# Moving row statistics, two attention loads and two weight splits to other steps of a hand-ordered layer kernel

## The chip, the cores and the metric

The kernel runs on one core of a Trainium2 chip. The core has five engines that work side by side, each through its own list of instructions in order: TensorE (PE, matrix products; PEld is its weight load), VectorE (DVE), ScalarE (ACT), GpSimd (POOL) and SyncE (SP), which here does nothing but issue transfers. Transfers are issued from SP's list and from ACT's list, as two queues, and are carried by the same 16 DMA engines. The metric is the device time of one execution in microseconds (us), lower is better; the median over several runs is compared.

## The reference

Input x has 2048 rows of 512 numbers, all float32. What is computed, cut to what matters:

```
xn  = layernorm(x)                                   # per row, no scale
qkv = xn @ wqkv                                      # 512 -> 3*512; 32 heads of 16
logits[s, w] = q[s] . k[s - 2w] / 4,  w = 0..7       # positions before 0 masked
o   = sum_w softmax(logits)[s, w] * v[s - 2w]
att = o @ wo
h   = relu(xn @ w1 + b1) ** 2                        # 512 -> 1792
g   = silu(h @ w2 + b2)                              # 1792 -> 512
out = x + att * g
```

## The kernel before

**Tiles and pairs.** The rows are cut into 16 tiles of 128 rows, which are worked in pairs (a, a+1). The first part of the program (up to about 139 us) makes q, k and v of all tiles; the second part runs the two wide layers over four chunks of 512 rows. The sliding attention of unit u (256 rows, so a pair of tiles) runs on VectorE beside both parts.

**One pair.** Each factor is split into a high and a low part in float32r, so that a product takes three passes. For pairs 4 to 14 the three 256-row products are made from seven products instead of eight, by `pair_of_seven` (L788): in order Q0, T1, T2, Q1, T3, K1, T4, with their partial sums kept in PSUM tiles `pm{a}_0` to `pm{a}_2`; pairs 6 to 12 do the same for half of v (`pv{a}_…`, in between). Pair 14 (the last) does v the plain way and also starts the wide layer (`ph0_0`, `ph0_1`). ScalarE copies each partial sum out before TensorE may add the next product onto it: the copy `pm{a}_1<-pm{a}_0` stands between Q0 and T2, and the copy `stg{a}_0<-pm{a}_0` of T3's result stands between T3 and T4. T1, T2, T3 and K1 use `S{a}_0` and `S{a}_1`, sums of transposed pieces: VectorE makes `Sf{a}`, ScalarE the high part of `S`, VectorE the low part (`low_sums`, L535).

**How a tile gets there.** `spread(t)` (L426) makes the statistics of a tile with two activations of ScalarE (they write a `waste` tile) and three small GpSimd operations; `norm(t)` (L441) then writes the normalised rows `xn`, and after the second tile of a pair `shuffle(t)` (L467) sends the pair through four transfers to `xb`, and loads the x tiles of a later pair. From `xb` VectorE transposes 32x32 blocks into PSUM (`pxT`), ScalarE copies the high part `xt`, VectorE makes the low part.

**What sets the order.** Inside a pair there are six steps; after each, `beside(a, step)` (L764) emits what the table `plan` holds for that place. `slots` (L746) says for each pair t where its statistics and its normalisation stand: four places (a, step), two for `spread` of t and t+1, two for `norm` of t and t+1, the transfers to `xb` with the last. `ahead` (L762) says where the splits of the wide layers' weights (`next_w`, L402: high parts on ScalarE, low parts on GpSimd, then the load of the weights two further on) stand. Every engine keeps program order, so what is emitted first on an engine runs first there. The transfers `sx` (a tile of xt to DRAM for the wide layers) are issued at the head of each pair (L876); `sk`, `sv`, `sq` carry a pair's k, v and q to DRAM from four staging buffers `stg`, so that a staging tile can be filled only when an older store has landed.

**The attention's place.** `attention()` (L248) is a generator that `pump` (L379) advances whenever the program's own clock of VectorE is behind that of TensorE. Its loads of a unit's k, q and v (`load`, L330) come back from DRAM on ACT's queue; they are put off by `defer` until the program's clock has passed a given time, and are emitted at the next `pump`. For unit 0, v's load may follow only from pair 4, step 3 on (`v_ready`).

Of the kernel before, what the change touches and what calls it, by code (L numbers as in the profile page):

```python
# [1 line left out]

# [49 lines left out]

MATMUL, VMATMUL, TRANSPOSE, DVE_FIXED, SHARED, SLACK, LATE, ROOM0, ROOM = 227, 120, 150, 150, 200, 500, 3000, 500, 3500

BEHIND, FAR, FREE, LAND, LOAD = 5000, 9000, 2000, 4500, 10500


@with_exitstack
def body(ctx: ExitStack, tc: tile.TileContext, x, wqkv, wo, w1, b1, w2, b2, out):
# [3 lines left out]
    clock = {"PE": 0.0, "V": 0.0}  # L63
# [30 lines left out]
    PE, V, A, G = Ordered(nc.tensor, "PE"), Ordered(nc.vector, "V"), Ordered(nc.scalar), Ordered(nc.gpsimd)  # L94

    def not_before(t):
        clock["V"] = max(clock["V"], t)
# [119 lines left out]
    def windows(t, i0, dims):  # L217

        part = t[:, i0]
        return bass.AP(tensor=part.tensor, offset=part.offset, ap=[part.ap[0], *dims])  # L220


    done_tiles = {n: [0, {}] for n in "qkv"}
    done_units = [0]

    def load_u(what, u):
        n = BI if what == "q" else WIN
        src = dict(q=sq, k=sk, v=sv)[what]

        t = att.tile([P, n, CH], F32, name=f"{what}{u}", tag="k" if (what, u) == ("v", NU - 1) else what)  # L230
        row = src[0, u * UP:u * UP + 1, :]
        ap = bass.AP(tensor=row.tensor, offset=row.offset, ap=[[BI * CH, NB], [src.shape[1] * CH, GR], [1, n * CH]])
        A.dma_start(t.rearrange("p i c -> p (i c)"), ap)
        return t
# [5 lines left out]
    def defer(t, f):  # L240
        behind.append((t, f))
        behind.sort(key=lambda b: b[0])

    def flush(t):
        while behind and (t is None or behind[0][0] <= t):
            behind.pop(0)[1]()

    def attention():  # L248

        tiles, Ls, landing, exps = {}, {}, {}, set()

        def qk(u, s):
            i0 = 4 * s
            yield from there("k", u)
            yield from there("q", u)
            q, k, L = tiles["q", u], tiles["k", u], Ls[u]
            yield 2350
            pr = att.tile([P, W, 2 * P], F32, name=f"pr{u}_{s}", tag="pr")  # L260
            qv = q[:, i0:i0 + 4, :].rearrange("p i c -> p (i c)")[:, None, :].to_broadcast([P, W, 2 * P])
            V.tensor_mul(pr, windows(k, i0, [[DIL * CH, W], [1, 4 * CH]]), qv)
            yield 2300
            V.tensor_reduce(
                out=L[:, s * 16:(s + 1) * 16, :].rearrange("p m w -> p w m"),
                in_=pr.rearrange("p w (g d) -> p w g d", d=HD), axis=AX.X, op=OP.add)

        def there(n, u):
            while (n, u) not in tiles:
                yield None  # L270
            not_before(landing[n, u])


        def part(u, h):
            n = BI * 4 // 2
            return slice(0, 2 * n) if h is None else slice(h * n, h * n + n)

        def soft_a(u, h=None):
            yield 1500 if h is not None else 700
            m = part(u, h)  # L280
            L, n = Ls[u][:, m], m.stop - m.start
            if u == 0:
                i = slice(m.start // 4, m.stop // 4)
                lm = L.rearrange("p (i h) w -> p i h w", h=4)
                V.tensor_add(lm, lm, mask[:, i, None, :].to_broadcast([P, n // 4, 4, W]))
            mx = att.tile([P, n], F32, name=f"mx{u}_{h}", tag="mx")
            V.tensor_reduce(out=mx, in_=L, axis=AX.X, op=OP.max)
            (G if h is None else V).tensor_sub(L, L, mx[:, :, None].to_broadcast([P, n, W]))

            def exp():  # L290
                A.activation(L, L, AF.Exp, scale=0.25)
                exps.add((u, h))

            defer(clock["V"] + (BEHIND if h is not None else FAR), exp)

        def soft_b(u, h=None):
            while (u, h) not in exps:
                yield None
            yield 2100 if h is not None else 1400
            m = part(u, h)  # L300
            L, n = Ls[u][:, m], m.stop - m.start
            sm = att.tile([P, n], F32, name=f"sm{u}_{h}", tag="sm")
            V.tensor_reduce(out=sm, in_=L, axis=AX.X, op=OP.add)
            V.reciprocal(sm, sm)
            (G if h is None else V).tensor_mul(L, L, sm[:, :, None].to_broadcast([P, n, W]))

        def av(u, s):
            i0 = 4 * s
            yield from there("v", u)
            v, L = tiles["v", u], Ls[u]  # L310
            yield 2400

            pr = att.tile([P, W // 2, 2 * P, 2], F32, name=f"pv{u}_{s}", tag="pr")
            vv = windows(v, i0, [[2 * DIL * CH, W // 2], [DIL * CH, 2], [HD, 16], [1, HD]])
            l = L[:, s * 16:(s + 1) * 16, :].rearrange("p m (a e) -> p a e m", e=2)
            V.tensor_mul(pr.rearrange("p a (g d) e -> p a e g d", d=HD), vv,
                         l[:, :, :, :, None].to_broadcast([P, W // 2, 2, 16, HD]))
            yield 2300
            V.tensor_reduce(
                out=v[:, i0:i0 + 4, :].rearrange("p i c -> p (i c)"), in_=pr.rearrange("p w n e -> p n w e"),  # L320
                axis=AX.XY, op=OP.add)

        def store(u):
            v = tiles.pop(("v", u))
            row = so[0, u * UP:u * UP + 1, :]
            dst = bass.AP(tensor=row.tensor, offset=row.offset, ap=[[BI * CH, NB], [S * CH, GR], [1, BI * CH]])
            dma(dst, v[:, :BI, :].rearrange("p i c -> p (i c)"))
            done_units[0] = u + 1

        def load(u, names):  # L330
            if u == NU:
                return
            for n in names:
                while done_tiles[n][0] < 2 * (u + 1):
                    yield None

                def start(n=n):
                    tiles[n, u] = load_u(n, u)
                    landing[n, u] = clock["PE"] + LOAD

                defer(max(clock["V"] + FREE if u else 0, done_tiles[n][1][u] + LAND), start)

        yield from load(0, "kq")

        for u in range(NU + 1):
            if u < NU:
                Ls[u] = att.tile([P, BI * 4, W], F32, name=f"L{u}", tag="L", bufs=2)
                for s in range(4):
                    yield from qk(u, s)
                    if u == 0 and s % 2:  # L350
                        yield from soft_a(0, s // 2)
                    if u == 0 and s == 1:
                        while not v_ready:
                            yield None
                        yield from load(0, "v")
                if u:
                    yield from soft_a(u)
                yield from load(u + 1, "kq")
                if u == NU - 1:
                    yield from load(u, "v")  # L360
            if u == 0:
                yield from soft_b(0, 0)
            for s in range(4):
                if u > 1 or (u == 0 and s < 2) or (u == 1 and s >= 2):
                    yield from av(max(u - 1, 0), s)
            if u == 0:
                yield from soft_b(0, 1)
            if u:
                store(u - 1)
                if u < NU - 1:  # L370
                    yield from load(u, "v")
                if u < NU:
                    yield from soft_b(u)

    v_ready = []
    stream = attention()
    coming = [None]

# [347 lines left out]
    def at(a, step, f, *args):  # L726
        if args[0] < NT:
            plan.setdefault((a, step), []).append((f, args))

    for a in range(2, NT, 2):  # L730
        n, t = {2: 2, 4: 1}.get(a, 0), a + 2
# [6 lines left out]
        if seven:  # L738
# [5 lines left out]
            at(a, n + 2 if n == 2 else n + 3 if n else n + 4, low_sums, t, 0)  # L744
            at(a, n + 3 if n else n + 5, low_sums, t, 1)
    slots = {6: ((2, 2), (2, 2), (2, 2), (2, 3)), 8: ((2, 4), (2, 5), (4, 0), (4, 1)),  # L746
             10: ((4, 5), (6, 0), (6, 1), (6, 2)), 12: ((6, 3), (6, 4), (6, 5), (8, 0)),
             14: ((8, 1), (8, 2), (8, 4), (8, 5))}
    for t, places in slots.items():
        for i, (a, step) in enumerate(places):  # L750
            at(a, step, norm if i > 1 else stats if t < STATS else spread, t + i % 2)
# [6 lines left out]
        at(a, step, f, n)  # L758
    for i in range(2):
        at(4, i, load_w, i)  # L760

    ahead = {(12, 3): 1, (12, 5): 1, (14, 0): 1, (14, 2): 1, (14, 4): 1}  # L762

    def beside(a, step):  # L764

        for f, args in plan.get((a, step), ()):
            f(*args)
        for n in range(ahead.get((a, step), 0)):
            next_w()
        if (a, step) == (4, 3):  # L770
            v_ready.append(True)
        pump(LATE)

    def pair(a):
# [185 lines left out]
    for c in range(NCH):  # L960
# [7 lines left out]
        for f in range(2, NF):  # L968
# [4 lines left out]
            if c == 0 and f in (3, 6):  # L973

                i = f // 6
# [67 lines left out]
        else:  # L1043
# [13 lines left out]
            for j in range(2, TPC):  # L1057
                n = D // 2 if j == TPC - 1 else D
# [25 lines left out]
```

## Time and profile before

| | us |
|---|---|
| median of 3 runs | 487.11 |
| lowest and highest run | 486.16, 488.63 |
| the profiled execution's own time | 487.94 |
| its span, from first to last instruction | 486.1 |
| TensorE busy in the span | 478.4 (98%) |
| VectorE, ScalarE, GpSimd busy | 422.6, 240.6, 224.8 |
| DMA engines over the span, mean rate | 168 GB/s |

The granted TensorE clock is full over the whole span. A profile page gives busy times over the whole span; the views used below cut it into stretches, list the instructions in order of time with the idle time before each and what ended it, follow back the chain of work that ended last, and give for a stretch the share of the 16 DMA engines that each queue held. In the last, q1 is the queue of SP's transfers and q10 that of ACT's. A line number in a row is mostly that of the helper that records every instruction (L90; L103 for transfers of SP), so rows are told apart by their tiles.

### The profile page before, as it was taken

How to read it: one execution, taken by the hardware profiler on the slowest of the kernel's cores; microseconds unless marked ns; L12 is line 12 of the kernel's file. 1: busy time of each engine (PE TensorE's matmuls, PEld its weight loads, DVE VectorE, ACT ScalarE, POOL GpSimd, SP SyncE). 2: the span in 40 equal slices, each digit the busy share in tenths (PEclk: the TensorE clock that was granted, in tenths of full speed). 3: DMA queues.
4: the chain of work that ended last, by engine and by line, in shares of the span. 5: the costliest groups of instructions: out<-in, count | busy, mean ns of one | idle time of the engine just before them, and what ended most of it. 6: DMA issues, size and time to landing. Idle time of an engine off the chain costs nothing.

```text
span 486.1 us, 6125 instructions
## 1 busy us (share of the span) xinstructions
PE 478.4 (98%) x2190; PEld 396.6 (82%) x2190; DVE 422.6 (87%) x352; ACT 240.6 (49%) x441; POOL 224.8 (46%) x178
## 2 busy tenths in 40 slices
PE   8999999999999999999999999999999999999996
PEld 5887888788888888888888888888888888888885
DVE  5968995989779899999999999999999999979133
ACT  5548798747475566264512444343234543423240
POOL 1358853215787599526543332443522335252210
PEclk9999999999999999999999999999999999999999
DMA  8899999997969997471618448181617734220322
GB/s 293 235 256 236 270 285 287 224 255 231 290 167 244 260 224 178 173 163 50 169 44 211 91 145 211 19 212 43 169 43 172 232 61 133 50 90 27 86 103 72
DMA packets 71002, 81.47 MB, mean 168 GB/s; under 512 B 6204, under 2 KB 55612, under 8 KB 70972
## 3 DMA queue, kind: packets, MB, share of 16 engines
q1 hardware_dynamic: 65788, 54.87, 40.8%
q10 hardware_dynamic: 5184, 26.22, 22.3%
q8 instruction: 17, 0.28, 0.2%
q14 instruction: 13, 0.11, 0.1%
HBM read 50.60 MB, written 27.32 MB: 160 GB/s over the span
## 4 chain that ended last, share of the span: by engine, by line
PE 78%; DMA 8%; DVE 6%; POOL 3%; ACT 2%; issue 2%; SPq 1%; ACTq 0%; DVEq 0%; POOLq 0%
PE pb L90 31%; PE ph L90 31%; PE pw L90 9%; DMA xb<-xn 4%; PE pq L90 4%; DMA x<-in_A_x 2%; PE pm L90 2%; DMA k<-sk 2%; POOL vsum L90 1%; DVE L L90 1%; POOL rs L90 1%; ACT stg L90 1%; ACT waste L90 1%; SPq L103 1%; DVE xt L90 1%
## 5 line engine op out<-in xcount | busy, mean ns | idle before, releaser
L90 PE MATMUL pb<-w,h 128*128 128x512 f32 x672 | 160.1, 389 | 0.0
L90 PEld LDWEIGHTS pb<-w,h 128*128 128x128 f32 x672 | 126.2, 188 | 26.1
L90 POOL TENSOR_TENSOR h<-hf,h 128x512 fp32r<-128x512 f32 x46 | 67.6, 1470 | 157.8 <-ACT hf L90 157.8
L90 PE MATMUL ph<-xU,w 128*128 128x512 f32 x504 | 120.2, 389 | 0.0
L90 ACT ACTIVATE ph<-ph,b1t 128x512 f32<-128x512 f32 x56 | 37.0, 661 | 154.6 <-PE ph L90 144.8
L90 PEld LDWEIGHTS ph<-xU,w 128*128 128x128 f32 x504 | 94.6, 188 | 19.6
L90 DVE TENSOR_TENSOR pr<-k,q 128x2048 f32<-128x2048 f32 x32 | 79.2, 2474 | 3.0 <-DMA q<-sq 2.3
L90 DVE TENSOR_TENSOR pv<-v,L 128x2048 f32<-128x2048 f32 x32 | 77.3, 2416 | 3.8 <-POOL L L90 3.1
L90 DVE TENSOR_REDUCE v<-pv 128x256 f32<-128x2048 f32 x32 | 73.0, 2280 | 0.7
L90 DVE TENSOR_REDUCE L<-pr 128x128 f32<-128x2048 f32 x32 | 73.0, 2281 | 0.7
L90 PE MATMUL pw<-wot,oT 128*128 128x512 f32 (+1 forms) x204 | 45.9, 376 | 0.0
L90 PEld LDWEIGHTS pw<-wot,oT 128*128 128x128 f32 x204 | 36.8, 188 | 7.1
L90 PE MATMUL ph<-xT,w 128*128 128x512 f32 x168 | 40.0, 389 | 0.0
L90 PE MATMUL pm<-wq,S 128*128 128x512 f32 x144 | 37.5, 395 | 1.1 <-ACT pm L90 0.5
L90 PEld LDWEIGHTS ph<-xT,w 128*128 128x128 f32 x168 | 31.5, 188 | 6.5
L90 ACT ACTIVATE h<-ph 128x512 fp32r<-128x512 f32 x56 | 33.7, 602 | 1.8
L90 POOL TENSOR_TENSOR w<-w1r,w 128x512 fp32r<-128x512 f32 x14 | 28.4, 2031 | 12.4 <-ACT w L90 9.6
L90 PEld LDWEIGHTS pm<-wq,S 128*128 128x128 f32 x144 | 25.9, 188 | 7.3 <-DVE S L90 1.9
L90 PE MATMUL pq<-wq,xT 128*128 128x512 f32 x132 | 30.8, 392 | 0.0
L90 PEld LDWEIGHTS pq<-wq,xT 128*128 128x128 f32 x132 | 24.5, 188 | 5.8 <-ACT xT L90 0.7
L90 PE MATMUL pm<-wq,xt 128*128 128x512 f32 x108 | 27.7, 393 | 0.8 <-ACT stg L90 0.8
L90 ACT ACTIVATE hf<-ph 128x512 f32<-128x512 f32 x46 | 27.3, 594 | 0.9 <-POOL h L90 0.9
(96 smaller groups left out, 533.4 us busy)
## 6 DMA issues: line engine op xcount, KB each, us to landing
k<-sk ACTq DMA_DIRECT2D x8, 960.0 KB, 7.2
v<-sv ACTq DMA_DIRECT2D x8, 960.0 KB, 7.6
sx<-xt SPq DMA_DIRECT2D x12, 512.0 KB, 5.9
xU<-sx ACTq DMA_DIRECT2D x12, 512.0 KB, 6.1
x<-in_A_x SPq DMA_DIRECT2D x16, 256.0 KB, 6.9
sk<-stg SPq DMA_DIRECT2D x8, 512.0 KB, 4.4
sq<-stg SPq DMA_DIRECT2D x8, 512.0 KB, 6.8
sv<-stg SPq DMA_DIRECT2D x8, 512.0 KB, 5.1
```

What stands on the lines that cost most here:

```text
L90: return tc.keep_in_program_order(f(*a, **k))
L103: tc.keep_in_program_order(dma(out, in_))
```

## The change

The table of places and the emission of two loads change; no instruction is added or removed.

```diff
-BEHIND, FAR, FREE, LAND, LOAD = 5000, 9000, 2000, 4500, 10500
+BEHIND, FAR, FREE, LAND, LOAD, APART = 5000, 9000, 2000, 4500, 10500, 6000
...
+    tiles, landing = {}, {}
+
+    def start(n, u):
+        tiles[n, u] = load_u(n, u)
+        landing[n, u] = clock["PE"] + LOAD
...
-            for n in names:
+            for i, n in enumerate(names):
                 while done_tiles[n][0] < 2 * (u + 1):
                     yield None
-
-                def start(n=n):
-                    tiles[n, u] = load_u(n, u)
-                    landing[n, u] = clock["PE"] + LOAD
-
-                defer(max(clock["V"] + FREE if u else 0, done_tiles[n][1][u] + LAND), start)
+                t = max(clock["V"] + FREE if u else 0, done_tiles[n][1][u] + LAND)
+                defer(t + (APART * i if u == 1 else 0), partial(start, n, u))
...
-                    if u == 0 and s == 1:
-                        while not v_ready:
-                            yield None
-                        yield from load(0, "v")
...
-             10: ((4, 5), (6, 0), (6, 1), (6, 2)), 12: ((6, 3), (6, 4), (6, 5), (8, 0)),
-             14: ((8, 1), (8, 2), (8, 4), (8, 5))}
+             10: ((4, 4), (6, 0), (6, 1), (6, 2)), 12: ((6, 3), (6, 3), (6, 5), (8, 0)),
+             14: ((8, 3), (8, 3), (8, 5), (10, 0))}
...
-    ahead = {(12, 3): 1, (12, 5): 1, (14, 0): 1, (14, 2): 1, (14, 4): 1}
+    at(8, 1, lambda u: start("v", u), 0)
+
+    ahead = {(12, 2): 1, (14, 0): 1, (14, 1): 1, (14, 2): 1, (14, 4): 1}
...
-        if (a, step) == (4, 3):
-            v_ready.append(True)
```

In words: the statistics of tile 10 stand one step earlier, those of 13 one step earlier, those of 14 and 15 two steps and one step later, the normalisations of 14 and 15 one step later each. Unit 0's v is loaded at pair 8, step 1; unit 1's q is put off by 6000 units of the program's clock behind its k. The split of weight 0 stands at pair 12, step 2 instead of step 3, that of weight 1 in pair 14 instead of pair 12, that of weight 2 one step later. The lists of all engines agree again from the first wide product on.

The first place is ScalarE in pair 8, from the statistics of tiles 14 and 15 (`waste14`, `waste15`) to the high part of `S10_0`; `stg8_0<-pm8_0` is the copy between T3 and T4. Before:

```order
L90 ACTIVATE waste14_981,mean14_978<-x14_823 128x512
L90 ACTIVATE waste14_981,rs14_979<-x14_823,mean14_978 128x512
L90 ACTIVATE stg8_2_911<-pv8_0_917 128x4x64
L90 ACTIVATE stg8_0_912<-pm8_1_914 128x8x64
L90 ACTIVATE stg8_2_911<-pv8_2_918 128x4x64
L90 ACTIVATE stg8_2_911<-pv8_1_916 128x4x64
L90 ACTIVATE waste15_1009,mean15_1006<-x15_825 128x512
L90 ACTIVATE waste15_1009,rs15_1007<-x15_825,mean15_1006 128x512
L90 ACTIVATE stg8_0_912<-pm8_0_913 128x8x64
L90 ACTIVATE stg8_2_911<-pv8_0_917 128x4x64
L90 ACTIVATE S10_0_1031<-Sf10_976 128x512
```

And now, with unit 0's v load at the head of the same piece:

```order
L91 DMA v0_976<-sv_150 128x1x1920
L91 ACTIVATE stg8_2_909<-pv8_0_915 128x4x64
L91 ACTIVATE stg8_0_910<-pm8_1_912 128x8x64
L91 ACTIVATE stg8_2_909<-pv8_2_916 128x4x64
L91 ACTIVATE stg8_2_909<-pv8_1_914 128x4x64
L91 ACTIVATE stg8_0_910<-pm8_0_911 128x8x64
L91 ACTIVATE stg8_2_909<-pv8_0_915 128x4x64
L91 ACTIVATE S10_0_1013<-Sf10_974 128x512
L91 ACTIVATE waste14_1020,mean14_1017<-x14_823 128x512
L91 ACTIVATE waste14_1020,rs14_1018<-x14_823,mean14_1017 128x512
L91 ACTIVATE waste15_1029,mean15_1026<-x15_825 128x512
L91 ACTIVATE waste15_1029,rs15_1027<-x15_825,mean15_1026 128x512
```

Four activations of statistics moved from ahead of the copy `stg8_0<-pm8_0` to behind it, and the v load came from the middle of pair 6 to this place.

The second place is SP's list at the head of pair 10, from the last store of pair 8 (`sq`) to the first of pair 10 (`sk`). Before:

```order
L103 DMA sq_148<-stg8_0_912 128x8x128
L103 DMA xb14_1075<-xn14_1055 32x4x256 x4
L103 DMA sx2_153<-xt10_946 512x1x256
L103 DMA sx2_153<-xt11_949 512x1x256
L103 DMA sk_149<-stg10_1_1086 128x8x128
```

And now:

```order
L104 DMA sq_148<-stg8_0_910 128x8x128
L104 DMA sx2_153<-xt10_944 512x1x256
L104 DMA sx2_153<-xt11_947 512x1x256
L104 DMA xb14_1123<-xn14_1072 32x4x256 x4
L104 DMA sk_149<-stg10_1_1080 128x8x128
```

The four transfers of tiles 14 and 15 to `xb14` moved behind the two `sx` transfers of 512 KB each.

The third place is ScalarE's list in pair 10, around the loads of unit 1's k and q. Before:

```order
L90 ACTIVATE Sf12_1147<-pxT13_1126 128x256
L90 DMA k1_1149<-sk_149 128x1x1920
L90 DMA q1_1151<-sq_148 128x1x1024
L90 ACTIVATE stg10_2_1087<-pv10_0_1093 128x4x64
L90 ACTIVATE stg10_0_1088<-pm10_1_1090 128x8x64
```

And now, with the same head and the piece around the q load:

```order
L91 ACTIVATE Sf12_1147<-pxT13_1120 128x256
L91 DMA k1_1149<-sk_149 128x1x1920
L91 ACTIVATE stg10_2_1081<-pv10_0_1087 128x4x64
L91 ACTIVATE stg10_0_1082<-pm10_1_1084 128x8x64
L91 ACTIVATE stg10_2_1081<-pv10_2_1088 128x4x64
L91 ACTIVATE stg10_2_1081<-pv10_1_1086 128x4x64
L91 ACTIVATE L0_339<-L0_339 128x256
L91 ACTIVATE stg10_0_1082<-pm10_0_1083 128x8x64
L91 ACTIVATE stg10_2_1081<-pv10_0_1087 128x4x64
L91 ACTIVATE S12_0_1190<-Sf12_1147 128x512
L91 DMA q1_1194<-sq_148 128x1x1024
```

The k load keeps its place; the q load moved behind eight more activations of the same pair.

More of the change, by code (lines that the diff above doesn't have):

```diff
@@ L1 @@
 from contextlib import ExitStack
+from functools import partial
 import concourse.bass as bass
@@ L246, in flush @@
             behind.pop(0)[1]()
+    tiles, landing = {}, {}
+    def start(n, u):
+        tiles[n, u] = load_u(n, u)
+        landing[n, u] = clock["PE"] + LOAD
     def attention():
-        tiles, Ls, landing, exps = {}, {}, {}, set()
+        Ls, exps = {}, set()
         def qk(u, s):
@@ L373, in attention @@
                     yield from soft_b(u)
-    v_ready = []
     stream = attention()
```

## The prediction

> **What bounds the kernel now.** I cut the span at the starts of the pairs first, TensorE alone (columns: stretch, its length, busy time and instructions, granted clock, DMA share, GB/s).
>
> ```profile
> core 0: us, PE busy (x), PEclk, DMA share, GB/s
> 57.07:72.49 15.42, 14.94 (x86) 1.00 0.94 263
> 72.49:88.27 15.78, 14.94 (x86) 1.00 1.09 273
> 88.27:103.37 15.10, 14.96 (x86) 1.00 0.97 213
> 103.37:118.05 14.68, 14.68 (x86) 1.00 1.00 315
> ```
>
> Pairs 6, 8, 10 and 12 run the same products. Pair 12 takes 14.68 us without a hole, so pair 6 loses 0.74, pair 8 1.10 and pair 10 0.42. The DMA engines are as full as TensorE: their share is near 1 in all four. The timeline of TensorE names the waits (in brackets: idle before, and what ended it).
>
> ```profile
> 61.86 1.65 PE L90 MATMUL pm<-wq,S 128*128 128x512 f32 x6 [0.48 <-ACT pm L90]
> 86.07 1.65 PE L90 MATMUL pm<-wq,xt 128*128 128x512 f32 x6 [0.84 <-ACT stg L90]
> 89.66 1.95 PE L90 MATMUL pm<-wq,S 128*128 128x512 f32 x6
> 119.44 0.61 PE L90 MATMUL pm<-wq,S 128*128 128x512 f32 x2
> ```
>
> Pair 6 waits at T2, pair 8 at T4 (both for a ScalarE copy); in pair 10 T1 is stretched; in pair 14 T1 starts at 119.44 and is cut after two products. The chain of waits tells why (start, length, what).
>
> ```profile
> 95.16 11.09 DMA xb<-xn
> 106.28 1.32 DVE pxT L90 x2
> 119.48 0.89 DVE S L90
> 120.41 1.20 PE pm L90 x4
> 121.61 2.74 PE pq L90 x12
> 127.08 5.44 PE ph L90 x24
> ```
>
> T1's six products should end at 119.44 + 1.36 = 120.8 (a whole group, 127.08 to 132.52, is 24 products in 5.44, so six take 1.36); pair 14 goes on at 121.61, 0.8 later. All four losses are 3.1 us, 0.6% of 487. Behind 121.61 TensorE is without a hole to its last product, so a microsecond saved or lost by then is one at the end. The chain shows what decides there: the last piece of `xb14` lands 11.09 after its issue, at 106.28, and VectorE then works its list without a stop until the low part of `S14_0` is done at 120.37: 14.1 us that no edit shortens. **The end of pair 14's T1 is the landing of `xb14` plus 14.1**, or TensorE's own arrival, whichever is later.
>
> **The change part by part.** Two terms are gains of ScalarE's order.
>
> ```profile
> 59.27 0.60 ACT L90 ACTIVATE stg<-pm 128x512 f32<-128x512 f32 x1 [1.12 <-POOL stg L90]
> 59.76 0.62 ACT L90 ACTIVATE waste<-x 128x512 f32<-128x512 f32 x1
> 61.23 0.58 ACT L90 ACTIVATE pm<-pm 128x512 f32<-128x512 f32 x1
> 82.93 0.60 ACT L90 ACTIVATE stg<-pm 128x512 f32<-128x512 f32 x1 [0.91 <-DMA sv<-stg]
> 83.95 0.64 ACT L90 ACTIVATE waste<-x 128x512 f32<-128x512 f32 x1
> 85.44 0.58 ACT L90 ACTIVATE stg<-pm 128x512 f32<-128x512 f32 x1
> ```
>
> Pair 6: tile 10's statistics take 61.23 - 59.76 = 1.47 between a copy that waited 1.12 for GpSimd and the copy that T2 needs. Moved ahead of that wait they start at 58.15, end at 59.6, and T2's copy ends near 60.6, before TensorE is there at 61.2. The 0.74 goes; what hides the statistics is the wait, and without it 1.47 - 1.12 = 0.35 would stay. Pair 8: tile 15's statistics (83.95 to 85.44) stand between the copy that waited for a store's landing and T4's copy; behind it, T4's copy ends near 84.5 even with the old landing, before TensorE at 85.1. The 1.10 goes.
>
> The third part is the load of unit 0's v, and here the transfers count. VectorE waited twice for `xb`, in pairs 8 and 12:
>
> ```profile
> 78.07 1.32 DVE L90 STREAM_TRANSPOSE pxT<-xb 128x512 f32<-128x512 f32 x2 [4.83 <-DMA xb<-xn]
> 106.28 1.32 DVE L90 STREAM_TRANSPOSE pxT<-xb 128x512 f32<-128x512 f32 x2 [2.27 <-DMA xb<-xn]
> ```
>
> and what the two queues got in 69 to 73, 97 to 102 and 102 to 106.3 (packets, MB, share of 16 engines) says who was ahead:
>
> ```profile
> q10 hardware_dynamic: 126, 0.94, 101.2%
> q1 hardware_dynamic: 35, 0.02, 3.0%
> ...
> q10 hardware_dynamic: 134, 0.98, 98.9%
> q1 hardware_dynamic: 55, 0.04, 6.8%
> ...
> q10 hardware_dynamic: 151, 0.52, 57.1%
> q1 hardware_dynamic: 474, 0.47, 44.1%
> ```
>
> The v load holds all engines for 4 us and SP's queue moves nothing meanwhile; unit 1's k does it for 5 us; its q (0.52 MB) shares 4.3 us. With v gone from 69, `xb10` lands some 4 us earlier (near 74), VectorE's 4.83 shrinks to about 1, and `S10_0` is ready before TensorE: the 0.42 goes too, which needs 2 of the 4 us. At its new place v is issued about 77.6 and served about 80 to 84; behind it stands `xb12`, which by the same sum lands near 88.5, and VectorE wants it near 89. TensorE then reaches T1 of pair 14 some 2.3 us earlier than before.
>
> The fourth part is `xb14`, and it can take all of it back.
>
> ```profile
> 89.94 1.35 SPq L103 DMA_DIRECT2D sq<-stg  x1
> 91.38 4.39 SPq L103 DMA_DIRECT2D xb<-xn  x4
> 94.67 0.52 ACTq L90 DMA_DIRECT2D k<-sk  x1
> 95.23 0.82 ACTq L90 DMA_DIRECT2D q<-sq  x1
> 95.81 1.38 SPq L103 DMA_DIRECT2D sx<-xt  x2
> DMA to landing us min/median/max: 13.1/13.1/13.1
> 90.00:92.00 2.00, 1.86 (x11) 1.41 (x10) 1.93 (x5) 0.79 (x2) 0.00 (x0) 1.00 1.05 283
> 108.00:110.00 2.00, 2.00 (x13) 1.77 (x12) 1.97 (x2) 0.86 (x2) 0.00 (x0) 1.00 1.14 349
> 73.00:78.00 5.00, 5.00 (x29) 4.38 (x28) 0.24 (x1) 4.53 (x10) 1.78 (x5) 1.00 1.09 191
> ```
>
> Before, three of the four `xb14` transfers were in front of k; the fourth fell behind k and q, and the two `sx` behind it landed 13.1 after their issue, the second near 96.5 + 13.1 = 109.6. Now the `sx` go first, and `xb14` takes the last place of this group of transfers. Three bounds for its landing. (a) If the group ends when it did, 109.6. (b) If the group starts with the pair, about 2 earlier: the three stores of pair 8 (1.57 MB at the 283 GB/s of 90 to 92: 5.5 us) from 88.6, when `xb12` is through, to 94.1, 0.2 of the 1.05 MB of `sx`, k alone from 94.7 (2.3 after an issue near 92.4) to 99.7, then q and SP's queue together to 104 (0.47 MB for SP, as above), then the rest of `sx` (0.38 MB at 349 GB/s: 1.1) and `xb14` (0.52 MB at the 191 GB/s of 73 to 78, when such transfers ran: 2.7): 107.8. (c) The same with q behind `xb14`: 99.7 + 0.85 MB at 349 (2.4) + 2.7 = 104.8. The q load is now issued after the high part of `S12_0`, by TensorE's advance near 97.5, seven us before (c) would be done, so it takes part of its 4.3 us in front; I take 106.5, nearest to the old 106.28.
>
> [...]
>
> The weight splits are the fifth part. Weight 0's high parts (two copies) now stand in front of T4's copy in pair 12, with TensorE waiting at pair 14 anyway; they cost nothing unless they last 2 us more. Its low parts leave GpSimd's list beside `S14_0`:
>
> ```profile
> 102.72 1.28 DVE L90 TENSOR_TENSOR S<-Sf,S 128x512 fp32r<-128x512 f32 x2
> 119.40 0.96 DVE L90 TENSOR_TENSOR S<-Sf,S 128x512 fp32r<-128x512 f32 x1
> ```
>
> Beside GpSimd's work one such operation took 0.96, alone 0.64 (two in 1.28): 0.3 off the 14.1. Weights 1 to 3 have TensorE's unchanged pair 14 to hide in: weight 1 is wanted at `ph0_1`, near 129.8, and its splits now end near 126.
>
> **Sum.** In the profiled execution (span 486.1, its time 487.94 with 1.8 around it) T1 of pair 14 moves by 106.5 - 106.28 - 0.3 = -0.1 us: the 2.3 gained in pairs 6 to 10 turns into a longer wait of VectorE for `xb14`, from 2.27 to about 5, and of TensorE in pair 14, from 0.8 to about 3. The profiled time is 0.8 over the median of the runs, which I take as base: 487.1 - 0.1 = 487.0.
>
> **The rivals.** *The whole gain is kept.* If `xb14` lands by 103.5, TensorE never waits for it: 487.1 - 3.1 = 484.0. For it: q is no longer right behind k, and the DMA engines idle in none of the four stretches for long, so an earlier start is an earlier end. Against: bound (c), which leaves q out altogether, is 104.8, 1.3 short; 104.1 already gives more than 0.5%. *`xb14` lands later (slower).* Its issue may slip: a store's issue took 1.35 at 89.94 with the queue full, and now stores and two `sx` stand in front. If the place of the last `sx` is not advanced at all, bound (a), the sum is 109.6 - 106.28 - 0.3 = +3.0: 490.1. It is slower by over 0.5% from a landing of 109.0 on. For it: the v load, moved to 80, fills the transfers right before this group. Against: all issues of the group follow TensorE, which is earlier. *The change does not do what it says*, that is, pairs 6 and 8 go on waiting: the copies' order speaks against it, and pair 14 would still set the end: 487.
>
> **How the numbers follow.** A measurement of this kernel tells 0.5%, 2.4 us, from no change (its runs lie 486.2 to 488.6). No change within that, `xb14` landing between 104.1 and 109.0, with the last rival in it: 0.50. The whole gain or most of it: 0.26. Slower: 0.24. The likeliest case has the range 485.3 (bound c) to 488.3 (bound b). The full range reaches to the whole gain and nearly to bound (a): 484.2 to 489.7.
>
> **What would show it.** TensorE's pairs 6, 8 and 10 at 14.7 each without the two waits on ScalarE; VectorE's wait in pair 8 at 1 to 2 us instead of 4.83; its wait for `xb` in pair 12 longer than 2.27, with a landing 8 us or more after issue; pair 14's T1 cut for 2 us or more. The prediction is wrong if VectorE's second wait is gone (then 484) or if its landing is past 109, and wrong in its base if TensorE gets a new hole behind 127.

## The result, and the profile after

| | before | changed |
|---|---|---|
| median of 14 runs each, us | 488.30 | 490.25 |
| lowest and highest run | 486.16, 494.74 | 488.09, 493.62 |
| the profiled execution's own time | 487.94 | 489.5 |
| its span | 486.1 | 487.7 |

The ratio is 1.0048, with a 95% interval of 1.0025 to 1.0072: the changed kernel is slower by about 2.3 us (the two medians differ by 1.95). 487.0 and no change had been forecast.

TensorE's pairs 8, 10 and 12 in the changed kernel (columns: stretch, its length, busy time and instructions, granted clock, DMA share, GB/s) are now dense:

```profile
71.53:86.21 14.68, 14.68 (x86) 1.00 1.06 289
86.21:100.89 14.68, 14.68 (x86) 1.00 1.11 291
100.89:115.57 14.68, 14.68 (x86) 1.00 0.84 237
```

Pair 14 begins at 115.57 instead of 118.05, 2.5 us earlier. Its timeline on TensorE (in brackets: idle before, and what ended it):

```profile
118.91 0.70 PE L91 MATMUL pm<-wq,S 128*128 128x512 f32 x2 [1.79 <-DVE stg L91]
120.35 1.46 PE L91 MATMUL pm<-wq,S 128*128 128x512 f32 x4 [0.74 <-DVE S L91]
121.60 4.28 PE L91 MATMUL pq<-wq,xt 128*128 128x512 f32 x12
125.72 1.54 PE L91 MATMUL pm<-wq,S 128*128 128x512 f32 x6
```

All that was won is waited away in two rests of 1.79 and 0.74 us. The chain of waits of the changed kernel (start, length, what) names the cause, the same as before:

```profile
95.31 10.90 DMA xb<-xn
...
106.40 1.32 DVE pxT L91 x2
...
119.70 0.61 DVE S L91
...
120.35 1.46 PE pm L91 x4
121.81 4.08 PE pq L91 x12
125.88 2.74 PE pm L91 x12
```

`xb14` landed at 106.2, as before, and T1 ended at 121.81, 0.20 later than the 121.61 of before. But the twelve products of `pq14_2` behind it took 4.08 us, where they took 2.74: another 1.34. 0.20 + 1.34 = 1.54 of the 1.6 us between the two profiled spans. A cut of that place into short stretches, TensorE alone, shows why:

```profile
118.90:121.60 2.70, 1.95 (x6) 0.91 0.81 235
121.60:123.00 1.40, 1.40 (x5) 0.50 1.06 298
123.00:124.00 1.00, 1.00 (x4) 0.50 0.98 275
124.00:125.00 1.00, 1.00 (x4) 0.74 1.03 289
125.00:126.00 1.00, 1.00 (x6) 1.00 1.04 319
```

The granted clock fell to half. Its shortfall adds up to 0.5 + 1.4 + 1.0 + 0.5 = 3.4 us at half speed (the first and fourth stretch by their means: 2.70 x 0.09 / 0.5, 1.00 x 0.26 / 0.5). The kernel before has the full clock at this place:

```profile
121.60:123.00 1.40, 1.40 (x8) 1.00 0.60 179
```

### The profile page after: what moved, and what is told of

The parts are those of the page before. It is cut to its first block, busy times and chain, and to the rows that moved or that the text cites. A ratio compares the mean times of both kernels' runs of the same rounds, so it can differ in the third digit from the quotient of the medians.

```text
span 487.7 us, 6129 instructions
## 1 busy us (share of the span) xinstructions
PE 479.3 (98%) x2190; PEld 398.0 (82%) x2190; DVE 423.7 (87%) x352; ACT 240.4 (49%) x441; POOL 232.3 (48%) x178
## 4 chain that ended last, share of the span: by engine, by line
PE 92%; DVE 3%; DMA 3%; SPq 0%; issue 0%; ACT 0%; POOL 0%; ACTq 0%; DVEq 0%; POOLq 0%
PE ph L91 31%; PE pb L91 31%; PE pq L91 9%; PE pw L91 9%; PE pm L91 9%; PE pv L91 2%; DMA xb<-xn 2%; DMA x<-in_A_x 1%; DVE v L91 0%; DVE pr L91 0%; DVE pv L91 0%; SPq L104 0%; PE pxT L91 0%; DVE pxT L91 0%; DVE xt L91 0%
## 5 line engine op out<-in xcount | busy, mean ns | idle before, releaser
L91 POOL TENSOR_TENSOR h<-hf,h 128x512 fp32r<-128x512 f32 x46 | 75.7, 1645 | 147.0 <-ACT hf L91 147.0
L91 DVE TENSOR_TENSOR pr<-k,q 128x2048 f32<-128x2048 f32 x32 | 80.9, 2528 | 3.5 <-DMA q<-sq 2.8
L91 POOL TENSOR_TENSOR w<-w1r,w 128x512 fp32r<-128x512 f32 x14 | 29.5, 2106 | 29.2 <-ACT w L91 29.2
```

Source lines behind the costliest of these rows:

```text
L91: return tc.keep_in_program_order(f(*a, **k))
```

## The experiments

Twelve kernels ran, in three groups; each ratio is to the kernel before, on the same chip in the same group, with its 95% interval. The first four ask what the hole, its length and its cause are worth.

**Filling the hole.** Eleven needless products on a partial sum that Q0 then overwrites stand at the head of pair 14; the rest is the changed kernel.

```diff
+        if last:
+            for n in range(11):
+                tc.keep_in_program_order(nc.tensor.matmul(
+                    sums_ps, part_x(a, 0)(0, 0), wq[Q0][:, 0, 0], start=n == 0, stop=n == 10, skip_group_check=True))
         product(sums_ps, part_x(a, 0), Q0)
```

> The changed kernel with 11 extra products ahead of pair 14's Q0, into the same PSUM tile, which Q0 then overwrites: 2.5 us of TensorE work where it rests. Nothing else moves, and xb14 should land near 106.4 again. Theory A (the granted clock fell to 0.50 because TensorE rested 1.79 and 0.74 us close together): the clock stays 1.00, pair 14's first v product takes 2.7 us and not 4.1, pair 14 goes on 1.5 us earlier, 1.5 us (0.3%) less than the changed kernel. Theory B (that product is slow by itself, from transfers and GpSimd work that now lie beside it): it still takes 4 us and the time is that of the changed kernel.

489.29 us, ratio 1.0024 (1.0002 to 1.0045). The filled kernel's TensorE timeline, and a stretch of its clock:

```profile
120.79 1.20 PE L91 MATMUL pm<-wq,S 128*128 128x512 f32 x4 [0.44 <-DVE S L91]
121.82 2.89 PE L91 MATMUL pq<-wq,xt 128*128 128x512 f32 x12
172.49 3.01 PE L91 MATMUL ph<-xT,w 128*128 128x512 f32 x12 [0.18 <-DVE h L91]
```

```profile
121.60:123.00 1.40, 1.40 (x8) 1.00 1.09 295
```

T1 ends at 121.98, no earlier than without the fill, so the end of pair 14's T1 hangs on `xb14` and not on TensorE. The clock stays full, `pq14_2` is back to its old length, and the first wide product starts at 127.43 instead of 128.62: 1.2 us won. By the ratios only about half of the loss went away, though, and the two intervals overlap. Behind 172 there is a wait that neither kernel of the comparison showed: from the first wide product to the group of products with the output weights (`pw`) near 327, TensorE took 201.5 us where both took 199.9. Here are the two ends of this way, first in the kernel before, then in the filled one:

```profile
126.92 4.47 PE L90 MATMUL ph<-xT,w 128*128 128x512 f32 x19
326.83 2.88 PE L90 MATMUL pw<-wot,oT 128*128 128x512 f32 x12
...
127.26 5.60 PE L91 MATMUL ph<-xT,w 128*128 128x512 f32 x24
328.79 2.88 PE L91 MATMUL pw<-wot,oT 128*128 128x512 f32 x12
```

The first `pw` group stands earlier, at 204.44 and 206.39, and shows the same 1.6 us. This was new and was followed up (below).

**`xb14` ahead of the two `sx`.** Only the normalisations of tiles 14 and 15 go back to their old places.

```diff
-             14: ((8, 3), (8, 3), (8, 5), (10, 0))}
+             14: ((8, 3), (8, 3), (8, 4), (8, 5))}
```

> The changed kernel with the normalisation of tiles 14 and 15 one step earlier each (pair 8, steps 4 and 5), so that xb14 is issued ahead of the two sx again. Theory A (xb14 was late because it stood behind sx, k and q): issues near 89.5 to 92, lands before 100, VectorE waits for it under 0.5 us, no hole in pair 14, clock 1.00, span near 483: 3 us (0.6%) under the kernel before. Rival (k takes the engines from whatever SP has queued, wherever it stands): the last piece still lands after k, at 102 or later, and some of the hole stays.

485.75 us, ratio 0.995 (0.993 to 0.997), span of the profiled run 482.9. This kernel's timeline of VectorE at the landing, and its chain in pair 14:

```profile
101.67 1.32 DVE L91 STREAM_TRANSPOSE pxT<-xb 128x512 f32<-128x512 f32 x2 [0.30 <-DMA xb<-xn]
```

```profile
115.72 2.75 PE pm L91 x12
118.47 2.72 PE pq L91 x12
```

`xb14` lands 4.7 us earlier than in the changed kernel, TensorE has no rest in pair 14, and this execution keeps all of the gain; by the ratio it is 2.4 us. One line of the table turns the change from slower into faster than the kernel before.

**That line alone, on the kernel before.**

```diff
-             14: ((8, 1), (8, 2), (8, 4), (8, 5))}
+             14: ((8, 1), (8, 2), (8, 5), (10, 0))}
```

> The kernel before with only the normalisations of tiles 14 and 15 at the changed kernel's places, so xb14 is issued behind the two sx, with k and q where they were. Theory A: xb14 has the last place of the group and lands near 109.6 instead of 106.3; pair 14's T1 waits some 3 us longer, the clock falls behind the hole, and the time is 3 to 5 us (0.6 to 1%) over the kernel before. Rival (xb14's landing is set by k and q alone): it lands near 106 to 107 and the time is within 1 us of before.

495.32 us in four runs, ratio 1.0136 (1.01 to 1.0172), more than expected; the mean granted clock is at most 0.995 in each of the four. Its timeline on VectorE and TensorE, and two stretches of its clock:

```profile
109.53 1.32 DVE L90 STREAM_TRANSPOSE pxT<-xb 128x512 f32<-128x512 f32 x2 [6.84 <-DMA xb<-xn]
...
121.64 0.70 PE L90 MATMUL pm<-wq,S 128*128 128x512 f32 x2 [2.99 <-DVE stg L90]
123.85 2.01 PE L90 MATMUL pm<-wq,S 128*128 128x512 f32 x4 [1.51 <-DVE S L90]
172.91 3.06 PE L90 MATMUL ph<-xT,w 128*128 128x512 f32 x12 [1.38 <-DVE h L90]
```

```profile
125.00:126.00 1.00, 1.00 (x4) 0.50 1.01 265
126.00:127.00 1.00, 1.00 (x4) 0.50 1.17 351
```

With k and q of unit 1 still together, `xb14` lands at 109.3, near bound (a) of the prediction. Three costs add up: rests of 2.99 + 1.51, the half clock behind them, and waits for `h` behind 172.

**q of unit 1 later still.** `APART` becomes 9000, and the program's estimate of q's landing is corrected by the 3000, so that VectorE's order stays.

```diff
-BEHIND, FAR, FREE, LAND, LOAD, APART = 5000, 9000, 2000, 4500, 10500, 6000
+BEHIND, FAR, FREE, LAND, LOAD, APART = 5000, 9000, 2000, 4500, 10500, 9000
...
-        landing[n, u] = clock["PE"] + LOAD
+        landing[n, u] = clock["PE"] + LOAD - (3000 if (n, u) == ("q", 1) else 0)
```

> The changed kernel with unit 1's q issued after the last copies of pair 10 (near 101.5 instead of 96.9), the rest of the order kept. Theory A (q shares the engines with what stands before it in time): xb14 lands near 104.8, 1.6 us earlier than in the changed kernel, pair 14's hole is 1 us or less, the clock stays at or near 1.00, and the time is 2 to 3 us under the changed kernel. Rival (k and sx alone set the landing): it lands near 106.4 as in the changed kernel and the time is the same.

487.21 us, ratio 0.998 (0.9958 to 1.0001). q is issued at 101.17 instead of 96.90, and VectorE's row of the landing reads

```profile
104.47 1.32 DVE L91 STREAM_TRANSPOSE pxT<-xb 128x512 f32<-128x512 f32 x2 [3.09 <-DMA xb<-xn]
```

So the part of q that went ahead of `xb14` cost 1.9 us, and bound (c), 104.8, was near. The rests are 0.46 and 0.73, and the clock stays full behind them (1.00 in every stretch from 115 to 130).

The second group asks what the parts of the change do.

**The splits back at their old places**, without and with the fill:

```diff
-    ahead = {(12, 2): 1, (14, 0): 1, (14, 1): 1, (14, 2): 1, (14, 4): 1}
+    ahead = {(12, 3): 1, (12, 5): 1, (14, 0): 1, (14, 2): 1, (14, 4): 1}
```

> The changed kernel with the three weight splits back at their old places; everything else of the change stays. Theory A (the hole of pair 14 and the low clock behind it are the slowdown; the splits only shorten GpSimd's list beside S14_0): xb14 lands near 106.3 again, the low part of S14_0 takes 0.96 instead of 0.61, the clock falls to 0.5 again, span 487.7 to 488.3, time as the changed kernel's or 0.3 over it. Theory C (the moved splits are themselves a cost, because weights are loaded later and the transfers of 130 to 140 shift to 140 to 165, into the q load): 1 to 2 us under the changed kernel, and the DMA share of 130 to 140 back from 0.37 to 0.6.

> The changed kernel with the eleven products that fill the hole and with the old places of the splits. The fill alone kept the clock at 1.00 and put the first wide product at 127.43 instead of 128.62, but TensorE then lost 1.6 us between 172 and 195, waiting for h behind VectorE's wait for q. Theory C (that second wait comes from the moved splits): it is gone here, T1 of pair 14 ends near 122.2, the first wide product starts near 127.6, span 486.7, time 1.2 under the filled kernel. Theory D (it comes from the lateness of the whole pair 14 against the store and load of q, or varies from run to run): span 487.5 to 488.5 with the same waits behind 172, or no waits in this execution and the same median.

492.06 us, ratio 1.005 (1.0024 to 1.0076), and with the fill 490.26, ratio 1.0029 (1.0005 to 1.0053): beside 1.0048 and 1.0024 no difference that these intervals can tell (for the first, the quotient of the two medians, 492.06 and 488.78, is 1.0067). Nothing was won back, so theory C falls, and no effect of the splits is shown. The waits behind 172 stayed in the second one (201.5 us from `ph` to `pw`), as theory D has it. The profiled execution of the first is one of the few with a hole and the full clock behind it (TensorE's timeline, then a stretch):

```profile
118.62 0.70 PE L91 MATMUL pm<-wq,S 128*128 128x512 f32 x2 [1.10 <-DVE stg L91]
120.85 1.20 PE L91 MATMUL pm<-wq,S 128*128 128x512 f32 x4 [1.52 <-DVE S L91]
```

```profile
122.00:123.00 1.00, 1.00 (x6) 1.00 0.71 234
```

Rests of 2.62 in all did not lower the clock here; in 9 of the 12 runs of this kernel it was lowered (a mean over the span below 0.998).

**The loads alone** (the tables `slots` and `ahead` of before in the changed kernel) **and the statistics alone** (the places of the statistics of the change in the kernel before):

> The changed kernel with the old places of all statistics, normalisations and splits: only the loads of v and q are moved. Leaves the reasons for the waits in pairs 6 and 8 in place, as I read them: holes of 0.74 and about 1.1 stay; pair 10's 0.42 goes; xb10 lands near 74; xb14, with three of its four transfers ahead of k and q some 4 us later, lands near 104 or earlier, so VectorE's second wait shrinks and pair 14 has no hole. Sum of the steps: 0.42 + 0.8 = 1.2 under the kernel before. If instead pair 8's hole comes from the old landing of the stores alone, 2.3 under it.

> The kernel before with the statistics of tiles 10 and 13 to 15 at their new places, normalisations of 14 and 15 at the old ones, loads and splits as before. Pairs 6 and 8 lose their 0.74 and 1.10; pair 10's 0.42 stays since v still goes ahead of xb10. If xb14 moves with TensorE's advance it lands near 104.5 and pair 14 keeps its hole of 0.8: 1.8 under the kernel before. If its landing stays at 106.3 (k and q of unit 1 hold the queues until then), the hole is 2.6 and the clock falls: 1 to 1.5 over the kernel before.

The loads alone: 487.06 us, ratio 0.9966 (0.9944 to 0.9987), faster, and neither pair 6 nor pair 8 has a hole, though their statistics stand where they stood. The statistics alone: 489.97 us, ratio 1.0037 (1.0013 to 1.0061), slower, and pair 8 still has one. VectorE, ScalarE and TensorE in this last kernel:

```profile
77.91 1.32 DVE L90 STREAM_TRANSPOSE pxT<-xb 128x512 f32<-128x512 f32 x2 [4.81 <-DMA xb<-xn]
...
78.67 1.19 ACT L90 ACTIVATE xt<-pxT 128x512 fp32r<-128x512 f32 x2 [0.89 <-DVE pxT L90]
81.80 0.38 ACT L90 ACTIVATE stg<-pv 128x256 f32<-128x256 f32 x1 [1.67 <-DMA sk<-stg]
...
82.23 0.98 PE L90 MATMUL pv<-vsum,S 128*128 128x256 f32 x6 [0.89 <-ACT stg L90]
```

`xb10` is as late as before (4.81 us of waiting), ScalarE works behind it and then waits for a store's landing, and TensorE waits 0.89 for ScalarE, earlier in the pair than before. By these two profiles pair 8's hole goes with v's load, not with the place of the statistics. In the kernel with the statistics alone `xb14` landed at 107.4, later than before, and the first wide product started at 128.33 instead of 126.92; 3 of its 12 runs had a lowered clock.

The third group asks about the wait behind 172. In the filled kernel VectorE's row there was

```profile
163.37 2.29 DVE L91 TENSOR_TENSOR pr<-k,q 128x2048 f32<-128x2048 f32 x1 [4.14 <-DMA q<-sq]
```

VectorE makes `h` for the wide layer in the same list, so TensorE waits for what stands behind this product. q had been issued 4.1 us after k (152.65 and 148.57). **q ahead of k for unit 2**, in the filled, the changed and the best kernel and in the one before:

```diff
-                yield from load(u + 1, "kq")
+                yield from load(u + 1, "qk" if u == 1 else "kq")
```

> The filled kernel with unit 2's q loaded ahead of its k instead of behind (near 150 us). In the traces so far q's issue came at the landing of the w2r transfer issued some 3 us before it, which flew 3.1 to 3.6 us or, when k's load had taken hold of the engines in between, 4.8 to 5.2; in the filled kernel it was 5.2, q landed at 163.3, and TensorE lost 1.6 us between 172 and 195. Theory E (k overtakes w2r, and that is the second wait): w2r flies under 3.8 us in every execution, VectorE's product of k and q starts within 35 us of the first wide product, from the first wide product to the first product of the output weights TensorE needs 199.9 us as in the kernel before (201.5 in the filled one), span 486.4, median 1 to 1.5 under the filled kernel. Theory F (the bytes decide, the later of the two loads lands at 163 in any order): the same 1.6 us behind 172, median as the filled kernel.

> The changed kernel with unit 2's q ahead of its k, no fill. If the low clock behind the hole of pair 14 is what the changed kernel loses, and the second wait is hidden behind it: within 0.5 us of the changed kernel's place, 1.8 to 2.3 over the kernel before, granted clock under 0.998 in most runs. If the second wait decides in many of its runs: 0.8 to 1.5 under that.

> The kernel with xb14 ahead of sx (2.4 us under the kernel before), with unit 2's q ahead of its k. Theory E: executions in which k overtakes w2r are gone, span 482.9 to 483.5 in nearly all runs, median 0 to 0.8 lower, 2.4 to 3.2 under the kernel before. Theory F: no difference or slower by up to 1.

> The kernel before with unit 2's q ahead of its k alone. Theory E, if the second wait is part of the kernel before's own spread (its spans reach from 484.6 to 489 at full clock): the upper runs go, median 0.3 to 1 under the kernel before. Theory F: the same within 0.3 or slower.

| with q first | us | ratio (interval) | ratio without q first |
|---|---|---|---|
| filled | 488.67 | 1.0014 (0.999 to 1.0037) | 1.0024 |
| changed | 490.04 | 1.0027 (0.9999 to 1.0055) | 1.0048 |
| `xb14` ahead of `sx` | 485.48 | 0.9937 (0.9913 to 0.9961) | 0.995 |
| before | 487.35 | 0.9994 (0.9971 to 1.0017) | 1 |

In the filled kernel the wait behind 172 is gone (199.9 us from `ph` to `pw`, no rest of TensorE there): with q first, VectorE waits for k, and for 1.52 instead of 4.14:

```profile
161.79 2.29 DVE L91 TENSOR_TENSOR pr<-k,q 128x2048 f32<-128x2048 f32 x1 [1.52 <-DMA k<-sk]
```

So in these two executions the order of the two loads makes the second wait, as theory E has it, though not by its detail: in this execution the `w2r` transfer of the same moment flew 4.7 us, where under 3.8 had been expected. All four ratios moved down, by 0.06 to 0.21%, which no single one of these intervals can tell from nothing. The profiled execution of the changed kernel with q first is a clear case of the clock, in stretches of TensorE:

```profile
122.00:124.00 2.00, 2.00 (x5) 0.50 1.03 283
124.00:126.00 2.00, 2.00 (x7) 0.50 1.01 283
126.00:127.00 1.00, 1.00 (x4) 0.50 1.07 303
127.00:128.00 1.00, 1.00 (x4) 0.50 1.05 348
```

Its rests were 2.11 and 0.74, the low clock lasted some 6.8 us, and `pq14_2` took 4.65. The profiled execution of the kernel before with q first shows something else, which that edit (near 150 us) cannot have made:

```profile
103.77 1.32 DVE L90 STREAM_TRANSPOSE pxT<-xb 128x512 f32<-128x512 f32 x2 [1.19 <-DMA xb<-xn]
...
118.11 1.52 PE L90 MATMUL pm<-wq,S 128*128 128x512 f32 x6
119.47 2.88 PE L90 MATMUL pq<-wq,xt 128*128 128x512 f32 x12
```

With the lists of the kernel before up to there, there are executions in which `xb14` lands 2.5 us earlier than in the profiled one of the prediction, and pair 14 has no hole at all. Of the 2.5 us, 1.4 are an earlier issue (89.97 instead of 91.38 for the first of the four transfers), with TensorE 1.3 us ahead as well (pair 14 starts at 116.72 instead of 118.05); the last transfer also flew 10.0 instead of 11.1.

**The clock over all runs.** Three kernels with the moved loads leave the hole open with `xb14` behind `sx`: the changed one, that with the old splits and that with q first. Of their 38 runs, 28 had a mean granted clock below 0.998, and spans of 487.7 to 491.8; the other ten had 485.7 to 487.4, without overlap. With the fill, none of 36 runs was below 0.998, nor was any of the 97 runs of the kernel before in these three groups. The ten lie where the kernel before lies (median spans of 486.3 to 486.6 against 486.1 to 486.7). Within each of the three kernels the median span of the lowered runs is 2.3 to 3.9 us longer; their transfers may also have landed later, so this is not the price of the clock alone.

## Why the prediction was wrong

**The landing of `xb14` and the end of T1: right.** 106.21 against 106.5; T1 of pair 14 at 121.81 against 121.5. VectorE's waits for `xb` in the changed kernel moved as forecast: 0.20 where 4.83 had been (about 1 was forecast), and 5.02 where 2.27 had been (about 5):

```profile
73.16 1.32 DVE L91 STREAM_TRANSPOSE pxT<-xb 128x512 f32<-128x512 f32 x2 [0.20 <-DMA xb<-xn]
89.51 1.32 DVE L91 STREAM_TRANSPOSE pxT<-xb 128x512 f32<-128x512 f32 x2 [0.83 <-DMA xb<-xn]
106.40 0.73 DVE L91 STREAM_TRANSPOSE pxT<-xb 128x512 f32<-128x512 f32 x1 [5.02 <-DMA xb<-xn]
```

The low part of `S14_0` took 0.61 instead of 0.89, the 0.3 of the prediction. But the 0.3 did not shorten the way from the landing to the end of this part: that took 14.1 us again (106.21 to 120.31), since other steps of VectorE on this way changed too, `L<-L,sm` for one from 0.42 to 0.82. Of the prediction's bounds, (b) 107.8 and (c) 104.8 held the landing; with q still later it was 104.3.

**The step that failed: the price of the longer wait in pair 14.** The prediction let the 2.3 us won turn into a wait of "TensorE in pair 14, from 0.8 to about 3", and priced it by its length alone. The length came nearly as said, 1.79 + 0.74. What it missed is that TensorE's clock was lowered to 0.50 behind these rests: 1.34 us in `pq14_2` in the profiled execution, and with it the 0.26 by which the last four products of T1 lengthened (1.46 against 1.20). The three pairs of kernels with and without the fill give the price over many runs: 1.0048 against 1.0024, 1.0050 against 1.0029, 1.0027 against 1.0014, so 0.6 to 1.2 us. All three differences point one way, though the intervals of each pair overlap, and in the first two the second wait has taken part of the price back. The traces show the half clock (0.50) behind such rests for 3.4 us in the changed kernel, 6.8 with q of unit 2 first, and 3.4 in the kernel with the one line of `slots` alone. The sum of the rests does not decide it alone: 2.62 us, with the old splits, went without a drop in one profiled execution, and 2.53, in the changed kernel, had one. There, 1.79 and 0.74 with 0.70 us of products between were enough; from which rest on the clock falls, and what decides it, these runs do not show.

**The base.** The prediction stood on one execution, in which pair 14 had a hole of 0.8 and `xb14` came at 106.28. Where it comes at 103.8 there is no hole to lose again, and the changed kernel's wait is a loss of its own. The median of three runs, 487.1, was 1.2 under that of the 14, so 1.2 of the 3.25 us between 487.0 and 490.25 are this base and not the change. How often each landing occurs in the kernel before is not known from two profiles.

**"Behind 121.61 TensorE is without a hole": only just.** In a kernel that reaches the wide layer earlier than its q, the wait behind 172 takes 1.6 us back; it was found only once the fill had removed the clock's loss. Fill and q first together leave 1.0014 (0.999 to 1.0037), which cannot be told from 1 and so fits the forecast of no change for what is left: a late `xb14` with no other cost.

**Pairs 6, 8 and 10: right in sum, wrong in cause.** All are at 14.68. But pair 8's 1.10, put down to the statistics of tile 15, goes with v's load alone and stays, as 0.89, with the statistics alone. Pair 6's 0.74 is not shown to come from the statistics of tile 10 either: in the kernel with only the last line of `slots` changed that pair has no hole, with its ScalarE list as before.

**The rivals.** "`xb14` lands later" came nearest in time (490.1), by luck: `xb14` did not land later, and 1.2 us of the agreement are the base. The landing decided nonetheless, since the kernel with `xb14` ahead of `sx` keeps the gain (0.995: 2.4 of the 3.1 us), as the rival at 484.0 said for an early landing.

## What to carry to other kernels

A gain ahead of a fixed landing is not merely lost when the engine waits for it: in this kernel rests of 1.79 and 0.74 us cost more than their length, 1.6 us behind them in the profiled execution and 0.6 to 1.2 us between the kernels with and without the fill. Where such rests cannot be removed, needless products in their place kept the clock full here (1.00 behind them in the profiled execution, none of 36 runs with a mean below 0.998). Move work in a queue by what waits for its last piece: four transfers behind two larger ones cost some 4.5 us here (490.25 against 485.75, in two groups of runs), more than the 2.4 us that all other edits together gained. And take several profiles of the kernel before where its runs spread by 1%: one execution's hole need not be the next one's.

## What the runs showed of the hardware

The clock's drop after rests of under 2 us each was the surprise; the table has the profiled executions, by rests of TensorE in pair 14 (the first, and the one after two more products), with the runs of the same kernel whose mean granted clock was below 0.998.

| kernel | rests, us | granted clock behind | runs lowered |
|---|---|---|---|
| q of unit 1 later | 0.46, 0.73 | full (1.00) | 0 of 10 |
| statistics alone | 0.16, 1.54 | full (1.00) | 3 of 12 |
| old splits | 1.10, 1.52 | full (1.00) | 9 of 12 |
| changed | 1.79, 0.74 | half (0.50) for 3.4 us | 11 of 14 |
| changed, q of unit 2 first | 2.11, 0.74 | half (0.50) for 6.8 us | 8 of 12 |
| one line of `slots` alone | 2.99, 1.51 | half (0.50) for 3.4 us | 4 of 4 |

The second was that the same transfers, behind the same lists, landed 2.5 us apart in two executions (`xb14` at 103.8 and 106.3), 1.4 us of it by their issue and 1.1 by their flight. This may be a part of the 5.9 us by which the spans of the kernel before differ (484.1 to 490.0 in the third group); how large a part is not shown. With k first, the load of unit 2's q is issued 1.9 to 5.0 us behind it in the profiled executions; why, no trace here shows.
